# Gated linear attention and a hard-swish feed-forward on one core: output stores moved to the sync queue, and another order of all steps

## The chip, the cores and the metric

The kernel runs on one core of a Trainium2 chip. The metric is the device time in microseconds, as the median of several runs. The program is built on the host in one pass: a Python function issues instructions to five engines, and each engine executes its own instructions strictly in the order in which they were issued. The engines are TensorE (matrix products, called PE in the profile; its weight loads are PEld), VectorE (DVE), ScalarE (ACT), GpSimd (POOL) and SyncE (SP, which does nothing here but start transfers). They meet only through semaphores.

## The reference

Two blocks follow each other. The first is a recurrent attention with a decay for each channel; the second is a feed-forward block with a hard-swish gate. Inputs have 4 batches, 8 heads, 768 tokens and 48 channels a head; the second block sees 3072 tokens of 384 features, and has 2048 hidden features. The weights `w_in` and `w_out` arrive as float64.

```python
state = np.zeros((B, H, D, D))
for t in range(S):
    state = alpha[:, :, t, :, None] * state + np.einsum('bhd,bhe->bhde', k[:, :, t], v[:, :, t])
    y[:, :, t] = np.einsum('bhd,bhde->bhe', q[:, :, t], state)
x = y.transpose(0, 2, 1, 3).reshape(B * S, H * D)
h = x @ w_in
g = h * np.clip(h + 3.0, 0.0, 6.0) / 6.0
out = g @ w_out
```

## The kernel before, in words

**Tiling.** The 3072 tokens are cut into 24 chunks of 128 tokens (six a batch), and two chunks make a group of the feed-forward block (groups 0 to 11). In a chunk, the recurrence is written as matrix products: a running product of the decays (two scans on VectorE, steps `r` and `p`), scaled keys and queries (`k`, `q`), masked scores (`sc`, `m`), the product with the values (`yi`), the part that comes from the carried state (`yx`), and the update of that state (`u`, `sm`, `st`). Groups 0 and 1 (and group 0 in halves, by chunk) take the feed-forward block directly: `fa`, `fb` and `f` are the first product, `fr` and `fg` the gate, `b` the second product of group 0. From then on both products are done with fewer multiplications and more additions: `xc` and `y` form sums of inputs and weights, `M` are the twenty products of a group, `n` copies a product from PSUM, `o` sums them, `e` and `h` are the gate; `s` forms sums of gated values, `P` are the seven products of the second layer, `K` and `G` collect them, and `O` stores a quarter of the group's output.

**Weights.** [...] each weight is decoded from its two 32-bit words. The weights come in 16 slices (0 to 7 are `w_in`, 8 to 15 are `w_out`). Step `w.i` (function `load_weight`, line 172) loads slice i: four transfers for a slice of `w_in`, one for a slice of `w_out`. For slices 0 to 4, two of the four transfers are started from ScalarE's queue and two from SyncE's; all others are started from SyncE:

```python
queue = nc.scalar if i < 5 and p > 1 else nc.sync      # line 183
```

Decoding has four or five steps: `d1.i` (line 207) and `d2.i` (line 217) on ScalarE, `dx.i` (line 212) on ScalarE for slices 0, 1, 2 and 4 only, `d3.i` on VectorE (lines 224 to 231), and `d4.i` on GpSimd (line 238), after which the slice may be used. A slice i of `w_in` is what `fa.i`, `fb.i`, `f.0.i` and `f.1.i` multiply with. Raw words of slices 0, 1 and 2 have buffers of their own, which later slices use again; slices 3 and 4 lie in space that group 1's gated values take later.

**Loads and stores.** `la`, `lk`, `lq` and `lv` load decays, keys, queries and values of a chunk from SyncE's queue: one or two transfers for chunks 0 to 5, four (or eight for the values from chunk 8 on) later. `kw` and `kr` write keys to memory and read them back in another layout, also from SyncE. The results are stored by `so` (line 620, chunks 0 and 1) and `O` (line 817, groups 1 to 11: 44 stores), both from ScalarE's queue. A result lies in one of four small buffers (`oh`), which the next user may write when the store has landed.

**Order.** The order is written out by hand as one long string of 1665 words (from line 842). A word is a step with its chunk or group and its buffer: `d2.1` is `magnitude(1)`, `f.0.3.2` is the first product of group 0 with slice 3 into PSUM bank 2. The words are executed one by one, so the order of the words of one engine is the order of its instructions. Words of different engines beside each other say nothing about time; only the order on each engine and the semaphores do. `z.m.n` are n products of the identity that nobody uses, which keep TensorE busy while it has nothing else to do.

Of the kernel before, what the change touches and what calls it, by code (L numbers as in the profile page):

```python
# [8 lines left out]
FP = mybir.dt.float32  # L9
# [8 lines left out]
def kernel(  # L18
# [32 lines left out]
    nc = tc.nc  # L51
    B, H, S, D = q.shape
    NTOK, DM = out.shape
    C = 128
# [6 lines left out]
    G = 2  # L61
# [23 lines left out]
    v0 = consts.tile([C, H, 64], FP, tag="vfirst")  # L85
# [42 lines left out]
    st, sm = [], []  # L128
# [490 lines left out]
    def store(c):  # L619
        nc.scalar.dma_start(out=out[c * C : (c + 1) * C, :], in_=os_t.pop(c))  # L620
# [193 lines left out]
    def store2(g, i):  # L814
        row, col = PLACES[i]
        j = G * g + row
        nc.scalar.dma_start(out=out[j * C : (j + 1) * C, col * HD : (col + 1) * HD],
                            in_=oh_t.pop((g, i)))
# [17 lines left out]
    def run(words):  # L836
        for word in words.split():
            name, *at = word.split(".")
            steps[name](*(int(x) for x in at))

    with tc.manual_schedule():
        run("""la.0 z.3.5 lv.0.0 lk.1 lq.0 ta.0.0 lv.1.1 z.0.3 ca.0 r.0 lk.0 tk.1.1 la.1 p.0 tq.0.2
               z.0.8 la.2 q.0 lq.1 tk.0.3 z.0.2 k.0 lv.3.2 ta.1.0 sc.0.2.3 ca.1 la.3 r.1 ta.2.0 w.1
               z.0.3 ca.2 m.0 kb.0.0 z.0.2 ck.0 r.2 tq.1.2 yi.0.3 p.1 z.0.3 lq.2 cy.0 k.1 u.0.0 q.1
               lk.2 ta.3.3 sm.0 sc.1.1.2 ca.3 lk.3 p.2 d1.1 kb.1.0 w.0 m.1 st.1 d2.1 tq.2.3 dx.1
               z.0.1 q.2 yi.1.1 d3.1 tk.2.2 ck.1 yx.1 r.3 u.1.3 lq.3 cy.1 k.2 d4.1 tk.3.0 lv.2.0
               sm.1 sc.2.1.2 k.3 w.3 st.2 fa.1.0 d2.0 m.2 d1.0 kb.2.3 d3.0 fb.1 dx.0 p.3 tq.3.0 w.4
               z.1.2 ck.2 d4.0 q.3 fr.0.1.0 u.2.1 sc.3.2.3 fg.0.1 sm.2 fa.0.1 m.3 st.3 d2.3 d1.3
               kb.3.0 w.5 d3.3 fb.0 ck.3 u.3.1 fr.0.0.1 yi.3.2 d4.3 sm.3 d1.4 fg.0.0 yi.2.3 d2.4 w.2
               dx.4 yx.3 d3.4 yx.2 f.0.3.2 cy.3 d4.4 cy.2 d1.5 la.5 d2.5 f.1.3.3 fr.0.3.0 lq.5 d3.5  # L850
               la.4 d1.2 f.1.4.0 fg.0.3 lv.4.1 d4.5 d2.2 dx.2 w.6 d3.2 tq.5.0 fr.1.3.1 ta.4.1 d4.2
               fr.1.4.0 ta.5.2 fg.1.3 fa.4.1 ca.4 fg.1.4 ca.5 r.4 w.7 fa.2.2 r.5 f.0.5.3 p.4 d2.6
               d1.6 st.4 lq.4 fb.2 fr.0.5.1 d3.6 w.8 f.1.5.0 fr.0.2.0 d1.7 fg.0.5 d4.6 fg.0.2 d2.7
               tq.4.3 fr.1.5.1 f.1.0.3 d3.7 w.9 q.4 d4.7 f.1.6.2 fr.1.0.0 fg.1.5 d2.8 fg.1.0 p.5
               d1.8 w.10 f.1.7.0 d3.8 fr.1.6.1 d2.9 q.5 f.0.7.3 d4.8 d1.9 lk.4 fg.1.6 fr.1.7.0 d3.9
               w.11 f.0.6.2 fr.0.7.1 d2.10 fg.1.7 d4.9 d1.10 fg.0.7 tk.4.1 fr.0.6.0 d3.10 f.1.2.0
               w.12 k.4 d4.10 fb.4 fg.0.6 d2.11 fr.1.2.1 d3.11 sc.4.2.3 w.13 d1.11 fr.0.4.0 f.1.1.3
               fg.0.4 d4.11 m.4 d2.12 d1.12 kb.4.0 lk.5 d3.12 b.1.0.2 fr.1.1.0 ck.4 w.14 fg.1.1
               d4.12 d2.13 fg.1.2 b.0.0.1 d1.13 d3.13 w.15 u.4.1 tk.5.2 d4.13 sm.4 b.1.1 k.5 d2.14
               st.5 d1.14 d3.14 lq.6 sc.5.3.0 yi.4.1 m.5 lq.7 d4.14 b.1.2 d2.15 d1.15 d3.15 la.6  # L860
               yx.4 b.0.1 tq.6 d4.15 lv.5.2 y.6 la.7 b.1.3 y.5 y.1 y.7 lk.7 y.2 y.11 yi.5.2 bo.1 x.0
               so.1 b.0.2 lv.7.0 y.4 y.13 ca.6 yx.5 y.0 b.0.3 cy.5 r.6 la.8 bo.0 cy.4 x.1 y.3 lv.8.1
               P.1.0.3 s.1.0.0 s.1.1.1 P.1.3.0 xc.2.1 x.2 K.1.0 s.1.2.3 xc.2.3 tk.7 s.1.3.2 P.1.2
               K.1.1 y.10 y.8 P.1.1.2 y.9 y.16 xc.2.4 s.1.4 P.1.4 x.3 K.1.2 y.15 s.1.5 xc.2.5 P.1.5
               G.1.1.0 P.1.6 G.1.3.1 y.17 y.19 G.1.0.2 y.18 y.12 y.20 M.2.0.1 tq.7 G.1.2.3 M.2.15.2
               M.2.16 lv.6.2 n.2.0.8 xc.2.6 y.21 y.23 M.2.1 xc.2.0 lk.6 lq.8 tk.6 xc.2.7 M.2.7.0 k.6
               xc.2.8 ca.7 xc.2.9 xc.2.2 r.7 vh.8 n.2.1.9 M.2.2 O.1.2 n.2.7.10 o.2.4.0 p.6 ca.8 lq.9
               la.10 la.9 lk.8 lk.9 xc.2.10 kb.6.0 M.2.8 O.1.1 n.2.2.11 M.2.3 M.2.4 n.2.4.12 o.2.0.0
               k.7 y.14 q.6 e.2.0.0 h.2.0 M.2.18.3 M.2.17 M.2.5 n.2.5.13 ck.6 M.2.9 o.2.1.0 e.2.1.1
               kb.7.3 sc.6.2.1 M.2.10 ck.7 u.6.0 u.7.3 n.2.10.14 M.2.11 n.2.11.15 p.7 m.6 q.7  # L870
               sc.7.1.2 M.2.12 n.2.18.12 M.2.19 y.22 M.2.6.1 h.2.1 n.2.12.11 M.2.13 sm.6 r.8 y.24
# [140 lines left out]
```

## Time and profile before

| what | value |
|---|---|
| median of 3 runs (lowest to highest) | 555.63 us (554.13 to 557.94) |
| span of the profiled run | 554.3 us |
| instructions | 14864 |
| DVE busy | 474.6 us (86%) |
| ACT busy | 205.0 us (37%) |
| transfers | 52.82 MB, 95 GB/s in the mean |

An engine's row gives the time in which it executed something, its share of the span, and the number of its instructions. TensorE's row counts the `z` products too. The mean hides the stages: memory traffic is near 200 GB/s in the first 95 us, where the weights come in, and near 100 GB/s later; VectorE is above 90% from 110 to 350 us.

### The profile page before, as it was taken

The page shows a single profiled execution, that of the slowest core. Times are in us where ns is not written, and L with a number is a line of the kernel's source. Part 1 is how long each engine was busy: PE and PEld are TensorE (multiplying, and loading weights), DVE is VectorE, ACT ScalarE, POOL GpSimd, SP SyncE. Part 2 cuts the span into 40 slices and gives each one's busy share as a digit, 9 for nine tenths or more (in the row PEclk, how much of TensorE's full clock was granted, in tenths as well). Part 3 has the DMA queues.
Part 4 walks back from the last instruction along what each step waited for, and adds up shares of the span by engine and source line. Part 5 has one row for each costly group of instructions (what it writes and reads, how often), then busy time and mean ns, then how long its engine had stood idle before and what let it go on. Part 6 is the DMA issues. An engine that isn't in the chain of part 4 may idle for free.

```text
span 554.3 us, 14864 instructions
## 1 busy us (share of the span) xinstructions
PE 539.9 (97%) x6222; PEld 512.7 (93%) x6222; DVE 474.6 (86%) x822; ACT 205.0 (37%) x358; POOL 56.1 (10%) x76
## 2 busy tenths in 40 slices
PE   8989999999999999999999999999999999999997
PEld 8789886699999899899999999999899899999997
DVE  6978997999999999899999998897899678756381
ACT  2487672104342332252251343333324333233230
POOL 3334346000100000000100000000100100000000
PEclk9999999999999999999999999999999999999999
DMA  8998678232303355343444434053234310000001
GB/s 176 200 200 172 197 240 211 57 73 67 81 0 80 96 127 136 97 119 94 99 117 109 101 84 110 26 136 99 62 86 116 88 33 8 8 31 2 10 19 44
DMA packets 98515, 52.82 MB, mean 95 GB/s; under 512 B 51472, under 2 KB 91664, under 8 KB 98448
## 3 DMA queue, kind: packets, MB, share of 16 engines
q1 hardware_dynamic: 90704, 45.18, 34.5%
q10 hardware_dynamic: 7744, 6.69, 4.1%
q8 instruction: 49, 0.80, 0.6%
q14 instruction: 18, 0.15, 0.1%
HBM read 43.71 MB, written 8.13 MB: 94 GB/s over the span
## 4 chain that ended last, share of the span: by engine, by line
PE 84%; DVE 6%; DMA 5%; issue 2%; ACT 1%; SPq 1%; ACTq 0%; POOL 0%; DVEq 0%; POOLq 0%
PE m_ps L796 32%; PE m_ps L693 29%; PE m_ps L571 6%; PE m_ps L609 4%; PE t_ps L549 2%; DMA v<-in_v_dram 2%; DMA out_dram<-oh 2%; PE m_ps L582 1%; PE t_ps L383 1%; DVE g_sb L630 1%; PE t_ps L408 1%; PE t_ps L529 1%; PE t_ps L314 1%; PE t_ps L533 1%; PE m_ps L625 1%
## 5 line engine op out<-in xcount | busy, mean ns | idle before, releaser
L796 PE MATMUL m_ps<-w,g_sb 128*128 128x192 f32 x704 | 121.5, 326 | 0.0
L796 PEld LDWEIGHTS m_ps<-w,g_sb 128*128 128x128 f32 x704 | 113.8, 190 | 0.4
L699 ACT COPY g_sb<-m_ps 128x512 f32<-128x512 f32 x110 | 63.9, 584 | 130.5 <-PE m_ps L693 108.6
L796 PE MATMUL m_ps<-rings,g_sb 128*128 128x192 f32 x528 | 91.4, 326 | 0.0
L693 PE MATMUL m_ps<-xc,w 128*128 128x128 f32 x640 | 83.7, 278 | 2.0 <-DVE oh L812 1.2
L796 PEld LDWEIGHTS m_ps<-rings,g_sb 128*128 128x128 f32 x528 | 85.3, 190 | 0.2
L587 ACT ACTIVATE r<-g_sb,half 128x512 f32<-128x512 f32 x80 | 56.7, 722 | 73.2 <-DVE g_sb L634 41.9
L693 PEld LDWEIGHTS m_ps<-xc,w 128*128 128x128 f32 x640 | 78.0, 192 | 4.3 <-DVE oh L812 1.4
L591 DVE SCALAR_TENSOR_TENSOR g_sb<-r,g_sb 128x512 f32<-128x512 f32 x80 | 53.7, 681 | 5.5 <-ACT r L587 4.4
L471 POOL TENSOR_TENSOR t<-t,R 128x384 f32<-128x384 f32 x20 | 21.8, 1088 | 360.4 <-DVE t L509 153.7
L693 PE MATMUL m_ps<-xT,raw 128*128 128x128 f32 x400 | 51.6, 276 | 0.7 <-DVE g_sb L632 0.7
L693 PEld LDWEIGHTS m_ps<-xT,raw 128*128 128x128 f32 x400 | 48.3, 192 | 1.4 <-DVE g_sb L632 1.0
L740 DVE TENSOR_TENSOR g_sb<-g_sb 128x512 f32<-128x512 f32 (+1 forms) x55 | 42.7, 802 | 2.5 <-PE m_ps L796 2.3
L693 PE MATMUL m_ps<-xT,w 128*128 128x128 f32 x320 | 42.3, 276 | 0.0
L693 PEld LDWEIGHTS m_ps<-xT,w 128*128 128x128 f32 x320 | 39.5, 192 | 0.2
L630 DVE TENSOR_TENSOR g_sb<-g_sb 128x512 f32<-128x512 f32 x40 | 27.8, 700 | 7.4 <-ACT g_sb L699 7.4
L341 DVE TENSOR_TENSOR_SCAN R<-t,ones 128x516 f32<-128x516 f32 x24 | 30.0, 1249 | 3.4 <-ACT t L332 2.0
L571 PE MATMUL m_ps<-xT,w 128*128 128x256 f32 x144 | 32.3, 381 | 0.0
L693 PE MATMUL m_ps<-xc,raw 128*128 128x128 f32 x240 | 32.1, 277 | 0.0
L352 DVE TENSOR_TENSOR_SCAN P<-t 128x516 f32<-128x516 f32 x24 | 30.3, 1262 | 0.1
L571 PEld LDWEIGHTS m_ps<-xT,w 128*128 128x128 f32 x144 | 26.9, 190 | 3.7 <-issue 0.2
L693 PEld LDWEIGHTS m_ps<-xc,raw 128*128 128x128 f32 x240 | 29.6, 192 | 0.5 <-issue 0.2
(121 smaller groups left out, 740.3 us busy)
## 6 DMA issues: line engine op xcount, KB each, us to landing
raw<-in_moe_w_out_dram SPq DMA_DIRECT2D x8, 768.0 KB, 4.4
out_dram<-oh ACTq DMA_DIRECT2D x44, 96.0 KB, 2.1
raw<-in_moe_w_in_dram SPq DMA_DIRECT2D x18, 192.0 KB, 4.2
qq<-in_q_dram SPq DMA_DIRECT2D x36, 96.0 KB, 2.6
aq<-in_alpha_dram SPq DMA_DIRECT2D x36, 96.0 KB, 2.6
kq<-in_k_dram SPq DMA_DIRECT2D x36, 96.0 KB, 2.5
far<-kq SPq DMA_DIRECT2D x13, 256.0 KB, 2.1
kb<-far SPq DMA_DIRECT2D x52, 64.0 KB, 2.2
```

The source lines that it names most:

```text
L341: nc.vector.tensor_tensor_scan(out=reverse(R, n - 1, n), data0=reverse(ax, n, n), data1=reverse(ones, n, n), initial=0.0, op0=ALU.mult, op ...
L352: nc.vector.tensor_tensor_scan(out=P_t[j], data0=aX[j % 2][:, 0:n], data1=ini[j % 2], initial=0.0, op0=ALU.mult, op1=ALU.add)
L471: nc.gpsimd.tensor_tensor(out=st[j % 2], in0=sm[j % 2], in1=R_t[j][:, :, 0:1].to_broadcast([C, NP, 2 * D]), op=ALU.mult)
L571: nc.tensor.matmul(h[:, f], w1[:, kk, o : o + C], xT_t[g][:, kk], start=(kk == 0), stop=(kk == KT - 1))
L587: nc.scalar.activation(out=to, in_=h, func=AF.Relu, bias=half, scale=1.0 / 6.0)
L591: nc.vector.scalar_tensor_tensor(out=to, in0=r, scalar=1.0, in1=h, op0=ALU.min, op1=ALU.mult)
L609: nc.tensor.matmul(o_t[c], gs[0][:, f, c * C : (c + 1) * C], w2[:, f], start=(f == 0), stop=(f == NF - 1))
L630: eng.tensor_tensor(out=out, in0=in0, in1=in1, op=ALU.add if s1 > 0 else ALU.subtract)
L693: nc.tensor.matmul(acc[g][i][:, f * C : (f + 1) * C], spots[w][:, f * C : (f + 1) * C], x_of(g, x), start=(first and f == 0), stop=last, s ...
L699: nc.scalar.copy(out=slots[z], in_=acc[g][i])
L740: nc.vector.tensor_tensor(out=out, in0=in0, in1=in1, op=ALU.subtract)
L796: nc.tensor.matmul(to[g], a, rhs[:, f], start=(first and f == 0), stop=(last and f == HF - 1), skip_group_check=True)
```

## The change

Two things are changed, and a name is given to one tile.

1. The output stores `so` and `O` are started from SyncE's queue in place of ScalarE's. They were the only transfers besides the halves of weight slices 0 to 4 that ScalarE started. The aim is that ScalarE no longer stands behind a result that another engine has yet to write.
2. All 1665 words stand in another order. It is the same set of steps, with some PSUM banks and buffers given out differently, and with the same 29 idle products, most of which now stand before the second transposition of keys. In the opening, chunks 0 to 3 are taken one after the other with the decoding of a weight slice between them; slice 0 comes first, and slice 4 only after slice 9.

```diff
@@ stores @@
-        nc.scalar.dma_start(out=out[c * C : (c + 1) * C, :], in_=os_t.pop(c))
+        nc.sync.dma_start(out=out[c * C : (c + 1) * C, :], in_=os_t.pop(c))
...
-        nc.scalar.dma_start(out=out[j * C : (j + 1) * C, col * HD : (col + 1) * HD],
+        nc.sync.dma_start(out=out[j * C : (j + 1) * C, col * HD : (col + 1) * HD],
                             in_=oh_t.pop((g, i)))
@@ the opening @@
-        run("""la.0 z.3.5 lv.0.0 lk.1 lq.0 ta.0.0 lv.1.1 z.0.3 ca.0 r.0 lk.0 tk.1.1 la.1 p.0 tq.0.2
-               z.0.8 la.2 q.0 lq.1 tk.0.3 z.0.2 k.0 lv.3.2 ta.1.0 sc.0.2.3 ca.1 la.3 r.1 ta.2.0 w.1
-               z.0.3 ca.2 m.0 kb.0.0 z.0.2 ck.0 r.2 tq.1.2 yi.0.3 p.1 z.0.3 lq.2 cy.0 k.1 u.0.0 q.1
-               lk.2 ta.3.3 sm.0 sc.1.1.2 ca.3 lk.3 p.2 d1.1 kb.1.0 w.0 m.1 st.1 d2.1 tq.2.3 dx.1
-               z.0.1 q.2 yi.1.1 d3.1 tk.2.2 ck.1 yx.1 r.3 u.1.3 lq.3 cy.1 k.2 d4.1 tk.3.0 lv.2.0
-               sm.1 sc.2.1.2 k.3 w.3 st.2 fa.1.0 d2.0 m.2 d1.0 kb.2.3 d3.0 fb.1 dx.0 p.3 tq.3.0 w.4
-               z.1.2 ck.2 d4.0 q.3 fr.0.1.0 u.2.1 sc.3.2.3 fg.0.1 sm.2 fa.0.1 m.3 st.3 d2.3 d1.3
-               kb.3.0 w.5 d3.3 fb.0 ck.3 u.3.1 fr.0.0.1 yi.3.2 d4.3 sm.3 d1.4 fg.0.0 yi.2.3 d2.4 w.2
-               dx.4 yx.3 d3.4 yx.2 f.0.3.2 cy.3 d4.4 cy.2 d1.5 la.5 d2.5 f.1.3.3 fr.0.3.0 lq.5 d3.5
...
+        run("""la.0 z.3.5 lv.0.0 lk.1 lq.0 ta.0.0 lv.1.1 z.0.3 ca.0 r.0 lk.0 tk.1.1 z.0.2 z.0.2
+               z.0.1 z.0.8 tk.0.2 p.0 k.0 tq.0.3 q.0 la.1 ta.1.0 ca.1 r.1 k.1 sc.0.2.3 m.0 p.1
+               kb.0.0 ck.0 u.0.1 sm.0 yi.0.0 lq.1 la.2 ta.2.2 tq.1.3 q.1 z.0.2 kb.1.1 w.0 ca.2 r.2
+               cy.0 ck.1 d2.0 d1.0 dx.0 lk.2 tk.2.2 k.2 sc.1.0.3 m.1 z.0.3 w.1 d2.1 st.1 kb.2.1
+               yi.1.2 u.1.0 yx.1 z.0.3 d3.0 d4.0 sm.1 d3.1 lq.2 lv.2.2 tq.2.3 fa.0.0 cy.1 ck.2 d1.1
+               u.2.0 la.3 ta.3.2 p.2 q.2 sc.2.1.3 m.2 st.2 dx.1 d4.1 ca.3 r.3 p.3 fb.0 fa.1.1 fb.1
+               w.2 d2.2 d1.2 dx.2 fr.0.0.0 d3.2 d4.2 lk.3 lq.3 tk.3.2 k.3 tq.3.1 q.3 yi.2.3 yx.2
+               sm.2 st.3 sc.3.2.1 m.3 w.3 la.5 fr.0.1.1 d2.3 d3.3 fg.0.1 d1.3 d4.3 kb.3.0 fa.2.2
+               lv.3.0 yi.3.1 yx.3 cy.3 fb.2 ck.3 u.3.2 sm.3 la.4 fr.0.2.1 cy.2 ta.4.1 ca.4 fg.0.2
+               r.4 fg.0.0 w.5 d1.5 d2.5 d3.5 d4.5 w.6 d2.6 d3.6 ta.5.0 f.0.3.3 f.1.0.1 fr.1.0.1
...
+               f.1.6.2 fr.1.6.0 d1.8 ca.5 r.5 f.1.3.1 f.0.6.0 fr.0.3.1 d4.8 w.9 d2.9 fg.1.6 k.4
+               fg.0.3 p.5 d1.9 d3.9 d4.9 fr.0.6.0 w.4 d2.4 d3.4 d1.4 dx.4 d4.4 fg.0.6 f.1.5.2
+               sc.4.1.2 m.4 f.0.7.3 kb.4.0 f.1.7.0 w.10 d2.10 d3.10 fr.0.7.1 fg.0.7 d1.10 d4.10 ck.4
+               fr.1.7.0 lv.4.1 u.4.3 sm.4 st.5 fg.1.7 fr.1.5.1 fg.1.5 w.11 d2.11 fr.1.3.0 d3.11
...
@@ one place in the middle @@
+               xc.6.7 m.14 h.5.2 xc.6.6 e.5.3.0 P.4.6 G.4.3.1 M.5.19 o.5.5.0 h.5.3 M.5.17 M.6.0.3
+               P.5.1.0 ca.16 sm.13 st.14 n.6.0.13 M.6.1 n.6.1.12 P.5.0.1 e.5.4.1 M.6.2 vh.14 yi.14.2
+               u.14.1 yx.14 kt.15 tq.15 p.15 h.5.4 r.16 e.5.6.0 h.5.6 o.5.7.1 la.18 lq.17 xc.6.8
+               s.5.0.8 n.6.2.11 e.5.5.1 M.6.7.2 e.5.7.0 K.5.0 h.5.7 M.6.3 M.6.4 h.5.5 s.5.1.15
+               s.5.2.9 G.5.0.2 tk.16 k.16 n.6.7.10 M.6.8 P.5.3.0 n.6.4.14 o.6.0.0 M.6.9 M.6.5 q.15
+               s.5.3.8 s.5.4 O.4.1 lv.15.1 kw.15 lq.16 kr.15 P.5.2 o.6.1.0 e.6.1.0 n.6.5.15 cy.14
+               e.6.0.1 xc.6.9 p.16 kt.16 sm.14 tq.16 s.5.5 q.16 h.6.0 ca.18 st.15 M.6.18.3 M.6.10
...
@@ the end @@
-               s.11.5 G.11.0.1 K.11.1 O.10.0 P.11.4 K.11.2 G.11.1.0 P.11.5 G.11.2.2 O.11.2 G.10.3.3
-               O.11.0 O.10.3 O.11.1 P.11.6 G.11.3.3 O.11.3""")
+               G.10.3.0 s.11.4 P.11.4 G.11.0.2 O.11.0 s.11.5 K.11.2 P.11.5 G.11.1.1 O.11.1 P.11.6
+               G.11.3.2 O.10.3 O.11.3 O.9.0 G.11.2.1 O.11.2""")
```

## The prediction

> **What bounds the kernel now.** I read the page first, then TensorE's waits, then the stretches, then the opening in order of time. The page says whose work fills the span:
>
> ```profile
> PE 539.9 (97%) x6222; PEld 512.7 (93%) x6222; DVE 474.6 (86%) x822; ACT 205.0 (37%) x358; POOL 56.1 (10%) x76
> PE   8989999999999999999999999999999999999997
> ```
>
> TensorE is the bound: 14.4 us of 554.3 are not filled. The step multiset is unchanged, so its work is too, and a new order can only change the gaps and what stands in place of the idle products `z`. The waits for the whole span show who ends TensorE's gaps; each is small:
>
> ```profile
> PE t_ps L549 <- issue: 2.5, 2, 1.3
> PE t_ps L494 <- ACT kb L437: 1.8, 2, 1.4
> PE m_ps L693 <- DVE oh L812: 1.2, 1, 1.2
> PE t_ps L529 <- ACT v L399: 1.0, 1, 1.0
> PE m_ps L693 <- ACT g_sb L699: 0.8, 1, 0.8
> ```
>
> The stretches (columns: length, then busy us of PE, PEld, DVE, ACT, POOL, clock, transfers) tell where:
>
> ```profile
> 10.00:20.00 10.00, 9.85 (x130) 8.46 (x128) 9.04 (x14) 3.65 (x6) 1.42 (x1) 1.00 0.94 201
> 20.00:30.00 10.00, 9.03 (x134) 7.60 (x133) 8.80 (x16) 5.93 (x7) 3.73 (x3) 1.00 1.10 205
> 30.00:40.00 10.00, 8.58 (x184) 8.04 (x186) 8.80 (x15) 7.83 (x10) 4.14 (x3) 1.00 0.85 187
> 40.00:50.00 10.00, 10.00 (x69) 8.82 (x61) 7.08 (x10) 9.30 (x13) 4.54 (x3) 1.00 0.97 192
> 300.00:350.00 50.00, 50.00 (x582) 49.13 (x584) 46.62 (x82) 17.83 (x35) 1.68 (x2) 1.00 0.40 97
> ```
>
> From 40 us on TensorE is full but for 6.8 us between 160 and 450 and the end. In the first 40 us it is idle for 4.0 and does about 8 us of `z` (29 products; 16 records, eight products, took 1.95), so some 12 us are lost there, while transfers run at 200 GB/s. VectorE at 93% in the last row has little to give. The full stretch begins with the first whole `f`:
>
> ```profile
> 40.37 8.04 PE L571 MATMUL m_ps<-xT,w 128*128 128x256 f32 x36
> ```
>
> What holds the opening is the weights' way through ScalarE (ACTq is a transfer started from ScalarE's queue):
>
> ```profile
> 18.01 0.32 ACTq L184 DMA_DIRECT2D raw<-in_moe_w_in_dram  x1
> 18.30 0.93 ACT L207 ACTIVATE raw<-raw 128x768 int32<-128x768 uint32 x1
> 19.76 0.40 ACTq L184 DMA_DIRECT2D raw<-in_moe_w_in_dram  x1
> ...
> 27.62 0.90 ACT L217 ACTIVATE w<-raw 128x768 f32<-128x768 f32 x1 [3.84 <-DMA g_sb<-in_moe_w_in_dram]
> 28.42 0.92 ACT L207 ACTIVATE raw<-raw 128x768 int32<-128x768 uint32 x1
> 29.37 1.93 ACT L212 ACTIVATE raw<-raw 128x768 f16<-128x768 int32 x1
> 29.38 0.88 ACTq L184 DMA_DIRECT2D g_sb<-in_moe_w_in_dram  x2
> ```
>
> Slice 0's halves leave at 18.01 and 19.76, and ScalarE stands for 3.84 until `d2.0` can start at 27.62. The last two lines also show that a transfer is started when the instruction before it begins, not when it ends.
>
> **What the Trainium skill says.** "DMA: Bandwidth & Descriptors", section on issuing engines: transfers from the scalar and sync queues run on the same 16 engines and interleave, so another queue saves only issue time. The trace agrees: transfers fill 0.94 to 1.10 of the engines in the rows above, whichever queue starts them. The same page, anatomy of one DMA: a wait for a semaphore is done by the sequencer that issues, ahead of dispatch; so a store that waits holds the loads behind it on SyncE. Before, ScalarE did this waiting (it stood 3.7 us for `oh` at L812 once between 160 and 460). Its rules for authors: start early, wait late; the 3.84 above is that rule broken once. "TensorE: Matmul & The Clock Gate", Part 1: after an idle window of about 3.4 us the clock falls to half. Here the longest gap in TensorE's row is 1.5 and the clock is 1.00, so no run shows it yet.
>
> **The change, part by part.**
>
> *The opening.* Up to its first whole `f` (`f.0.3`), the new order places all that the old one does ahead of its own (`f.0.3` too, at 40.4), and further `fa.2`, `fb.2` (1.34 each, spacing of L582), `ta.4`, `ta.5` (0.45 each): 3.6 us. It breaks even if `f.0.3` starts at 44.0. It needs slice 3. The halves of slices 0 to 4 from ScalarE's queue now stand directly ahead of their own decoding: `dx.0, w.1, d2.1` and `dx.1, ca.3, w.2, d2.2`; in the old order four ScalarE instructions stood between the start of slice 1 and its first decoding step, and four again for slice 0. Each landing is thus shown in full, in series with ScalarE. Landings of these halves took 3.1 to 7.4 us, median 5.5 from ScalarE's queue in the windows at 10 and 18 us, 5.0 at 26.
>
> - `k.0` ends at 10.7 as before, `q.0` at 11.3, `sc.0` (1.1) and `kb.0` (0.45) at 12.9; `ck.0` starts at 13.0 and `w.0` leaves at 13.1; landed 18.7.
> - `d2.0`, `d1.0` (0.92 each) to 20.6; `dx.0` starts and `w.1` leaves, landed 26.6 (two issues 0.5, landing 5.5).
> - `d2.1`, `cy.1`, `ck.2` (0.92, 0.46, 0.67), `d1.1` (0.92) to 29.6; `dx.1` starts and `w.2` leaves; landed (5.0) 34.8.
> - `d2.2`, `d1.2` to 36.7; `dx.2` starts, `w.3` leaves, landed 41.7.
> - `d2.3` (0.92), `d3.3` on VectorE (0.69, 0.69, 0.96) and `d4.3` on GpSimd (1.84): 46.9.
>
> So `f.0.3` starts near 47, 3.0 later than break-even. Behind the waiting `d2.1` stand `ck.2` (for `u.2`) on ScalarE, and behind `d3.1` the scan `p.2` on VectorE. With landings of 3.1 from `w.1` on it is 41, but then VectorE and TensorE set it, near 44: 0; with 7.4 it is +9. I take +3.0.
>
> *Slice 4* is loaded late, again with `d2.4` next. `fg.0.6` on VectorE stands behind `d3.4`, `ck.4` behind all of slice 4 and slice 10. From the end of `f.0.6`: landing 4 to 5, `d2.4`, `dx.4`, two `d2`/`d1`, `fr.0.7` come to some 11 us until `ck.4`; TensorE has `f.1.5`, `sc.4`, `f.0.7`, `kb.4`, `f.1.7` (3 x 2.59 + 1.1 + 0.45 = 9.3) ahead of `u.4`. +1.2 (0 to 2.6).
>
> *Stores on SyncE.* 44 issues of 0.34 leave ScalarE, which is 37% busy; what they can give is TensorE's waits for ScalarE after 160, 1.0 + 0.8: I take -1.0. They come to SyncE, whose four-part load takes 2.0 and eight-part load of values 5.3 to 8.0. Between `tq.15` and `tq.16` the new order has six `M` (0.89) and two `P` (2.60) on TensorE, 10.6 us; SyncE has `lq.17`, `O.4.1`, `lv.15`, `kw.15`, `lq.16` (2.0 + 0.4 + 5.6 + 0.4 + 2.0) and 2.6 to landing, 13.0. Late by 2.4, and about 1 more at `lv.8` by the same reckoning. VectorE waits, and in its wake TensorE: +2.0 (0 to 5).
>
> *The end.* The old last copy waited 0.5 (551.33 against 550.79) for a store; the new one takes a free buffer, but two stores follow the third last on the queue (0.4 each): +0.3. The tile's name costs nothing, it is in no instruction. Moving the `z` products costs nothing either: they fill the wait for `lk.0`.
>
> Sum: 3.0 + 1.2 - 1.0 + 2.0 + 0.3 = +5.5, hence 561.1.
>
> **The rivals.**
>
> *Faster (0.12).* ScalarE and the new order close the gaps from 160 to 450 (6.8), and the opening breaks even: 555.6 - 6.8 + 0.3 = 549. For it: each gap is small and ended by an engine the change relieves or reorders. Against: only 1.8 of it waits for ScalarE, and VectorE is as full as before.
>
> *Hidden (0.25).* Landings are short because SyncE has run out of other loads, slice 4 is covered, loads are in time: +0.3 to +2, about 556.5. For it: in the old trace transfers fall to a third of the engines near 33 us. Against: the 3.84.
>
> *A cold clock (0.11).* Between `fa.0` (about 25.8) and `u.2` (behind `ck.2`, 28.7) TensorE has 3 us with nothing; if this passes the skill's window, small products run at half speed for another such window, and with landings of 7.4: 555.6 + 9 + 2 + 3 = 569 at the outside.
>
> **How the numbers follow.** The main case has 0.52 and spreads over 556 to 567 about 561.1. 1% is 5.6 us, so 550.1 and 561.2 part the classes. The unknown costs of the main case reach further up (+9, +2.6, +5) than down, so I put 0.6 of it (0.31) above 561.2; with the cold clock that is 0.42 for slower. Same gets the rest of it and the hidden case, 0.46, and faster 0.12. The range of 552 to 569 leaves out most of the fast rival and what lies beyond the cold one.
>
> **What would show it.** In the changed profile: ScalarE's L217 waiting for a transfer of `raw` two to three times for 3 us or more in the first 45 us; the first L571 near 47; a gap at L494 near 28; small gaps near 80; VectorE's L318 waiting for `qq` near 300; ACT without waits for L812. The prediction is wrong if L571 starts before 44, or if TensorE's gaps after 160 sum to less than 4.

## The result, and the profile after

The changed kernel takes 563.4 us in the median of four runs (562.3 to 564.2), against 555.9 us (554.1 to 557.9) for the kernel before on the same chip: a ratio of 1.0132, 95% interval 1.0091 to 1.0174, so slower by about 1.3%. The profiled run has a span of 560.9 us, 6.6 more than before. Three views say where the 6.6 us went. First the page: the engines' row for TensorE, and the granted clock in 40 slices of 14 us.

```profile
PE 543.6 (97%) x6222; PEld 515.8 (92%) x6222; DVE 473.7 (84%) x822; ACT 203.8 (36%) x358; POOL 53.2 (9%) x76
PEclk9979999899999999999999999999999999999999
```

TensorE has the same 6222 products but is busy for 3.7 us more than before: the clock row has a 7 and an 8, slices in which the same work took longer. The stretches (from and to, length, then busy us of PE, PEld, DVE, ACT, POOL, clock, share and rate of the transfers) put the first of them into the opening:

```profile
10.00:20.00 10.00, 8.82 (x123) 7.55 (x122) 9.28 (x15) 2.73 (x5) 0.84 (x1) 1.00 1.17 218
20.00:30.00 10.00, 6.19 (x116) 5.02 (x113) 4.13 (x8) 5.90 (x7) 2.62 (x2) 1.00 1.11 219
30.00:40.00 10.00, 8.63 (x67) 8.11 (x62) 7.11 (x10) 5.69 (x6) 1.83 (x1) 0.66 0.89 198
40.00:50.00 10.00, 10.00 (x188) 9.02 (x187) 6.53 (x12) 5.49 (x10) 4.16 (x3) 1.00 0.71 156
```

Between 20 and 30 us TensorE is busy for only 6.2 us of 10 and VectorE for 4.1, where before they were at 9.0 and 8.8. So it is neither of them that sets the pace there. The two engines' own instructions say what they wait for: the timeline of ScalarE (its transfers are ACTq, the bracket is the idle time ahead and its releaser), then one line of VectorE's and TensorE's gaps with the first `f`:

```profile
13.54 0.86 ACTq L184 DMA_DIRECT2D raw<-in_moe_w_in_dram  x2
20.12 0.93 ACT L217 ACTIVATE w<-raw 128x768 f32<-128x768 f32 x1 [1.78 <-DMA raw<-in_moe_w_in_dram]
21.95 0.80 ACTq L184 DMA_DIRECT2D raw<-in_moe_w_in_dram  x2
27.83 0.89 ACT L217 ACTIVATE w<-raw 128x768 f32<-128x768 f32 x1 [3.94 <-DMA rings<-in_alpha_dram]
30.83 0.81 ACTq L184 DMA_DIRECT2D raw<-in_moe_w_in_dram  x2
37.03 0.91 ACT L217 ACTIVATE w<-raw 128x768 f32<-128x768 f32 x1 [4.25 <-DMA raw<-in_moe_w_in_dram]
38.80 0.92 ACTq L184 DMA_DIRECT2D g_sb<-in_moe_w_in_dram  x2
43.48 0.92 ACT L217 ACTIVATE w<-g_sb 128x768 f32<-128x768 f32 x1 [1.75 <-DMA g_sb<-in_moe_w_in_dram]
```

```profile
28.75 0.69 DVE L224 TENSOR_SCALAR w<-w 128x768 f32<-128x768 f32 x1 [5.63 <-ACT w L217]
```

```profile
25.85 1.60 PE L582 MATMUL m_ps<-xT,w 128*128 128x128 f32 x12 [1.63 <-POOL w L238]
29.63 0.56 PE L494 MATMUL t_ps<-v,kb 128*48 128x48 f32 x16 [2.18 <-ACT kb L437]
32.16 2.08 PE L408 MATMUL t_ps<-q,k 48*128 48x128 f32 x16 [1.37 <-DVE q L364]
...
50.21 13.12 PE L571 MATMUL m_ps<-xT,w 128*128 128x256 f32 x60
...
80.41 2.86 PE L571 MATMUL m_ps<-xT,w 128*128 128x256 f32 x12 [1.40 <-DVE g_sb L591]
83.69 0.56 PE L494 MATMUL t_ps<-v,kb 128*48 128x48 f32 x16 [0.42 <-ACT kb L437]
...
109.28 1.93 PE L539 MATMUL t_ps<-A,v 128*32 128x128 f32 x32 [2.81 <-DVE A L416]
```

Four pairs of ACTq and L217: half of a slice is started, and 4.7 to 6.6 us later its first decoding step begins. ScalarE has three short copies to do behind the first start, nothing behind the second and one or two instructions behind the others; for the rest it stands idle, 1.78, 3.94, 4.25 and 1.75 us. The releaser of 27.83 names another load; it is inferred, and what `d2.1` reads is slice 1. Behind this `d2.1` stand VectorE (5.63 us, for what `d2.1` writes) and then TensorE at 29.63 and 32.16; its gap ahead of 25.85 belongs to slice 0, whose last step `d4.0` was over only then (23.97 + 1.82). The first `f` comes at 50.21; at 44.0 the opening would have broken even.

The third view is TensorE's row of waits over the whole span (sum, times, longest):

```profile
PE t_ps L494 <- ACT kb L437: 3.3, 3, 2.2
PE t_ps L539 <- DVE A L416: 2.8, 1, 2.8
PE t_ps L408 <- DVE q L364: 1.9, 2, 1.4
```

The three longest rows are all made ahead of 110 us. Of the waits that stood at L693 and L529 before, none is left: behind 160 us the gaps sum to 0.7 us (0.23 and 0.48), where they were 6.8. So the new order loses in the first 136 us and wins in the rest:

| part | after against before, us |
|---|---|
| opening: first `f` at 50.21, even at 44.0 | +6.2 |
| gaps at 80 and 84 us (before: none) | +1.8 |
| gaps at 109 and 136 us (2.81, 0.17; before: none) | +3.0 |
| low clock from 110 to 114 us (2.0 at 0.50, 2.0 at 0.81) | +1.4 |
| gaps behind 160 us, 0.7 for 6.8 | -6.1 |
| from the last product's end to the end, 3.9 for 3.5 | +0.4 |
| sum (the spans differ by 6.6) | +6.7 |

The opening's share is that of one pair of profiles. Two other runs below have the same opening in the same order, with the first `f` at 50.71 and 51.85, so it is good to a microsecond or two.

### The profile page after: what moved, and what is told of

It is laid out like the page before. It is cut to its first block, busy times and chain, and to the rows that moved or that the text cites. A ratio compares the mean times of both kernels' runs of the same rounds, so it can differ in the third digit from the quotient of the medians.

```text
span 560.9 us, 14905 instructions
## 1 busy us (share of the span) xinstructions
PE 543.6 (97%) x6222; PEld 515.8 (92%) x6222; DVE 473.7 (84%) x822; ACT 203.8 (36%) x358; POOL 53.2 (9%) x76
## 4 chain that ended last, share of the span: by engine, by line
PE 75%; DVE 4%; DMA 2%; issue 1%; POOL 1%; ACT 1%; POOLq 0%; DVEq 0%; ACTq 0%
PE m_ps L796 33%; PE m_ps L693 33%; DMA raw<-in_moe_w_out_dram 2%; PE t_ps L549 2%; PE t_ps L383 2%; PE t_ps L529 2%; PE t_ps L533 1%; PE t_ps L488 1%; DVE rings L740 1%; POOL w L238 1%; PE t_ps L385 1%; DVE raw L630 1%; PE t_ps L539 0%; DVE raw L634 0%; ACT w L217 0%
## 5 line engine op out<-in xcount | busy, mean ns | idle before, releaser
L699 ACT COPY g_sb<-m_ps 128x512 f32<-128x512 f32 x110 | 63.6, 586 | 139.0 <-PE m_ps L693 120.0
L693 PE MATMUL m_ps<-xc,w 128*128 128x128 f32 x640 | 83.1, 277 | 0.0
L693 PEld LDWEIGHTS m_ps<-xc,w 128*128 128x128 f32 x640 | 78.1, 192 | 0.9 <-issue 0.2
L693 PE MATMUL m_ps<-xT,raw 128*128 128x128 f32 x400 | 52.1, 277 | 0.0
L471 POOL TENSOR_TENSOR t<-t,R 128x384 f32<-128x384 f32 x20 | 20.2, 1008 | 330.0 <-DVE t L509 192.1
L693 PEld LDWEIGHTS m_ps<-xT,raw 128*128 128x128 f32 x400 | 48.4, 192 | 0.8 <-issue 0.2
L693 PE MATMUL m_ps<-xT,w 128*128 128x128 f32 x320 | 42.5, 277 | 0.0
L693 PEld LDWEIGHTS m_ps<-xT,w 128*128 128x128 f32 x320 | 39.4, 192 | 0.7 <-issue 0.2
L693 PE MATMUL m_ps<-xc,raw 128*128 128x128 f32 x240 | 32.0, 276 | 0.0
L693 PEld LDWEIGHTS m_ps<-xc,raw 128*128 128x128 f32 x240 | 29.5, 192 | 0.6 <-issue 0.6
L630 DVE TENSOR_TENSOR g_sb<-m_ps,g_sb 128x512 f32<-128x512 f32 x30 | 20.6, 685 | 10.7 <-PE m_ps L693 6.3
```

What stands on the lines that cost most here:

```text
L471: nc.gpsimd.tensor_tensor(out=st[j % 2], in0=sm[j % 2], in1=R_t[j][:, :, 0:1].to_broadcast([C, NP, 2 * D]), op=ALU.mult)
L630: eng.tensor_tensor(out=out, in0=in0, in1=in1, op=ALU.add if s1 > 0 else ALU.subtract)
L693: nc.tensor.matmul(acc[g][i][:, f * C : (f + 1) * C], spots[w][:, f * C : (f + 1) * C], x_of(g, x), start=(first and f == 0), stop=last, s ...
L699: nc.scalar.copy(out=slots[z], in_=acc[g][i])
```

## The experiments

Ratios are against the kernel before, in runs on the same chip as each experiment.

### The stores' queue in the new order

```diff
-        nc.sync.dma_start(out=out[...
+        nc.scalar.dma_start(out=out[...
```

> The changed kernel with the output stores back on ScalarE's queue, order kept. Theory (the new order closed TensorE's gaps after 160 us, 6.8 to 0.7): gaps stay under 2, time 562 to 565. Rival (the queue of the stores closed them): gaps of 4 us or more come back, time 567 to 570.

575.0 us, ratio 1.0342 (1.0306 to 1.0377), 11.6 more than the changed kernel and more than either theory gave. Behind 160 us TensorE's gaps sum to 8.1 us in place of 0.7, so the order alone had not closed them. TensorE's waits have a new first row, and ScalarE's timeline shows one of its causes:

```profile
PE m_ps L693 <- ACT g_sb L699: 7.0, 4, 4.3
```

```profile
455.95 0.34 ACTq L817 DMA_DIRECT2D out_dram<-oh  x1
456.34 0.72 ACT L587 ACTIVATE r<-g_sb,half 128x512 f32<-128x512 f32 x1 [5.93 <-DVE oh L812]
456.96 0.57 ACT L699 COPY g_sb<-m_ps 128x512 f32<-128x512 f32 x1
```

The store that leaves at 455.95 had stood in ScalarE's row for the `oh` that VectorE had yet to write (5.93 us of idle time); behind it stands the copy at L699, which empties the bank that TensorE needs. The new order puts stores well ahead of their data; where SyncE does this waiting, as in the changed kernel, TensorE's 0.7 us of gaps show no cost.

### The stores' queue in the old order

```diff
-        nc.scalar.dma_start(out=out[...
+        nc.sync.dma_start(out=out[...
```

> The kernel before with the output stores on SyncE's queue alone, order kept. Theory (the queue matters little by itself): 554.5 to 558, gaps after 160 us of 5 to 8. Rival (the queue closes the gaps): 549 to 551. The prediction's fear (stores hold loads back on SyncE): 558 or more.

567.4 us, ratio 1.0208 (1.0165 to 1.0251): the time of the prediction's fear (558 or more), though it is a store that waits behind loads and not a load behind stores. One gap of 8.0 us that ends at 244 us and the clock after it (0.50 from 244 to 248 us) make most of the loss. ScalarE's line and SyncE's queue:

```profile
243.98 0.32 ACT L809 COPY oh<-m_ps 128x192 f32<-128x192 f32 x1 [10.50 <-DMA out_dram<-oh]
```

```profile
235.88 5.32 SPq L299 DMA_DIRECT2D v<-in_v_dram  x8
...
241.88 1.92 SPq L817 DMA_DIRECT2D out_dram<-oh  x4
```

The store stands behind the eight parts of a value load, the copy at L809 waits for its buffer, and L693 for the copy. Of the loss 3.1 us lies in the opening, where nothing was changed (first `f` at 43.48 against 40.37): openings of one order differ by so much between runs. So neither half of the change stands alone: moving the stores costs 12 us in the old order, the new order costs 12 us more without it. Neither queue is better by itself; the order has to be laid out for the queue that the stores are on.

### Late halves in the old order

The halves from ScalarE's queue were made a step of their own, `wa.i`, and put right ahead of the decoding of their slice in the old order: `wa.1` ahead of `d1.1`, `wa.0` of `d2.0`, `wa.3` of `d2.3`, `wa.4` of `d1.4`, `wa.2` of `d1.2`.

```diff
-            for p in range(NP):
-                queue = nc.scalar if i < 5 and p > 1 else nc.sync
+            for p in (range(2, NP) if second else range(2 if i < 5 else NP)):
+                queue = nc.scalar if second else nc.sync
```

> The kernel before, with the ScalarE-started halves of slices 0 to 4 each started right ahead of its own first decoding step on ScalarE, as the changed kernel has them; nothing else moves. Theory (late starts cost the opening): the first L571 at 44 to 48 us in place of 40.4, time 559 to 563. Rival: under 557, since transfers fill the memory engines anyway.

567.8 us, ratio 1.0214 (1.0168 to 1.0260): 12.6 us for five starts moved back, more than the theory gave. The first `f` comes at 45.75, 5.4 us later, as the theory said. ScalarE stands 5.58 and 5.86 us for the first steps of two slices, and TensorE behind it:

```profile
27.38 0.88 PE L494 MATMUL t_ps<-v,kb 128*48 128x48 f32 x16 [4.83 <-ACT kb L437]
...
52.64 7.69 PE L571 MATMUL m_ps<-xT,w 128*128 128x256 f32 x23 [4.03 <-ACT xT L557]
```

The late start alone is enough, in the old order, to lose what the change lost and more.

### Early halves in the new order, from ScalarE

The same split in the changed kernel, with `wa.0 wa.1` behind `w.0`, `wa.2 wa.3` behind `dx.0` and `wa.4` behind `ca.4`.

> The changed kernel, with the ScalarE-started halves of slices 1, 2, 3 and 4 started earlier on ScalarE (1 right behind 0, 2 and 3 behind dx.0, 4 behind ca.4); nothing else moves. Theory (the late starts make the opening's loss): the first L571 at 44 to 46 us in place of 50.2, no stretch at half clock near 33 us, the gap at 80 us gone, time 556 to 559. Rival (the chunk-by-chunk order, VectorE or memory traffic sets the opening, and the waits for landings only show it): L571 stays at 49 or later, time 562 or more.

559.9 us, ratio 1.0082 (1.0043 to 1.0121). The gaps at 80 us are gone, but the first `f` comes at 51.02, no earlier than in the changed kernel. That looks like a verdict against the late starts; the timeline of ScalarE shows that it isn't one:

```profile
12.87 5.68 ACTq L184 DMA_DIRECT2D raw<-in_moe_w_in_dram  x4
```

```profile
24.73 3.62 ACTq L184 DMA_DIRECT2D g_sb<-in_moe_w_in_dram  x2
28.45 0.89 ACT L217 ACTIVATE w<-raw 128x768 f32<-128x768 f32 x1 [4.32 <-DMA g_sb<-in_moe_w_in_dram]
```

In the changed kernel two such starts took 0.80 to 0.92 us; here it was 5.68 us from the first of four to the end of the last, and 3.62 us for two. ScalarE stood at the issue, and `d2.1` began 0.10 us after the issue was over. The wait for a landing had only been exchanged for a wait at the issue, at the same place. Slices 2 and 3 did come in time (`d2.2` starts at 33.33 without a wait), and TensorE has no gap from 32.77 us on; but its clock is 0.50 from 32 to 38 us, as in the changed kernel from 32 to 36, and `f` comes no earlier. How much of that is the stand ahead of `d2.1`, and how much the clock behind it, this run doesn't part. It mixed several things and left the question open; the next one is cleaner.

### All parts from SyncE's queue

```diff
-                queue = nc.scalar if i < 5 and p > 1 else nc.sync
+                queue = nc.sync
```

> The changed kernel with one line different: all four parts of slices 0 to 4 are started from SyncE's queue, at the places where SyncE's own two parts stand (8.7, 10.4, 16.1 and 20.3 us in the changed kernel's trace), so that ScalarE starts nothing and can't stand at an issue[...]. The same bytes move. Theory A (the late start of ScalarE's halves is what makes the opening long; starting them early from ScalarE had only put the issue's standing in place of the wait for the landing): the waits of 3.9 and 4.3 us ahead of d2.1 and d2.2 fall below 1.5, VectorE no longer stands 5.6 us ahead of d3.1, TensorE's gaps between 25 and 33 us (5.2) shrink to under 2.5 and with them the stretch at half clock; the first L571 comes at 44 to 47 us instead of 50.2, and the time is 557 to 561. Theory B (the opening is bound by the bytes of all loads, whichever is started first): the loads of chunks 2 and 3 come later by what the halves come earlier, new waits for k, q or v of chunk 2 take their place, the first L571 stays at 49 to 52, and the time is 562 to 565.

552.7 us, ratio 0.9958 (0.9941 to 0.9975), where the changed kernel had 1.0132: 1.7% less, or about 10 us (the two medians, from two chips, differ by 10.7), from one line that moves no byte less. SyncE's queue (slices 1 and 3), then ScalarE's L217 for slices 1, 2 and 3, then TensorE's first `f`:

```profile
11.04 2.12 SPq L184 DMA_DIRECT2D raw<-in_moe_w_in_dram  x4
...
24.05 4.78 SPq L184 DMA_DIRECT2D g_sb<-in_moe_w_in_dram  x4
```

```profile
21.10 0.94 ACT L217 ACTIVATE w<-raw 128x768 f32<-128x768 f32 x1
...
28.14 0.91 ACT L217 ACTIVATE w<-raw 128x768 f32<-128x768 f32 x1 [0.96 <-DMA raw<-in_moe_w_in_dram]
...
33.50 0.98 ACT L217 ACTIVATE w<-g_sb 128x768 f32<-128x768 f32 x1 [0.24 <-DMA g_sb<-in_moe_w_in_dram]
```

```profile
42.64 13.12 PE L571 MATMUL m_ps<-xT,w 128*128 128x256 f32 x60
```

Issues take as long here (2.12 and 4.78 us for four), but an engine stands at them that computes nothing. The waits of 3.94, 4.25 and 1.75 are down to none, 0.96 and 0.24; the clock is 1.00 throughout; the first `f` is 7.6 us earlier. The spread is small too: 552.0 to 553.9 in 20 runs, where the kernel before had 553.1 to 559.0 in 23. Theory A holds in the waits that it named, also against the reading of the run before it; the first `f` and the time came out better than it gave (44 to 47, 557 to 561). The two profiled spans differ by 9.4 us: the opening gives 7.6, the gaps at 80 us 1.8 and the clock at 110 us 1.4, and the gaps near 109 us take 0.6 back. Those stay in another form, 3.6 us between 99 and 126 us for 3.0, so they belong to the order and not to the halves.

### One slice at a time

```diff
-                queue = nc.scalar if i < 5 and p > 1 else nc.sync
+                queue = nc.scalar if i in (0, 2, 3, 4) and p > 1 else nc.sync
```

> The changed kernel with the parts of slice 1 alone all on SyncE; slices 0, 2, 3 and 4 keep their halves on ScalarE. It tells how the late starts add up. Theory A (each late landing costs by itself: slice 1's holds ScalarE's kb, VectorE's decoding and by the gaps the clock, 5 to 6 us; slices 2 and 3 some 2 more): the wait ahead of d2.1 and the half clock go, the waits ahead of d2.2 and d2.3 stay at 2 to 5 us, the first L571 comes at 45 to 47, the time is 557 to 560. Theory B (the latest of them alone sets the end, slice 3's landing): the opening hardly moves, the first L571 at 49 to 50.5, 562 to 564.

561.9 us, ratio 1.0104 (1.0045 to 1.0163), with runs from 559.2 to 563.3; the profile is of the lowest. In it `d2.1` has no wait, the opening keeps its clock, `d2.2` and `d2.3` still wait 4.60 and 3.21 us, and the first `f` comes at 46.33. So the opening behaved as theory A says, and the time of the median does not: 1.5 us of about 10. How much slice 1 is worth alone is not settled beyond "a part, and not all".

```diff
-                queue = nc.scalar if i < 5 and p > 1 else nc.sync
+                queue = nc.scalar if i == 4 and p > 1 else nc.sync
```

> The changed kernel with the parts of slices 0 to 3 on SyncE, and slice 4's half on ScalarE as in the changed kernel, started right ahead of its own decoding. Against the run with all five on SyncE (552.7) it gives the price of slice 4 alone. Theory A (my step for slice 4: 1.2, 0 to 2.6; the changed kernel's trace had gaps of 1.40 and 0.42 at 80 us behind a wait of 4.6): ScalarE waits 4 us or more for it near 70 us, TensorE's gaps of 1.4 to 2 us stand there again, and the time is 554 to 555. Theory B (those gaps were VectorE's, or the opening's delay carried on): no gap, 552 to 553.3.

555.8 us, ratio 1.0008 (0.9987 to 1.0029), against 0.9958 with slice 4 on SyncE too: 0.5%, or 2.8 us, for slice 4. ScalarE's lines and TensorE's:

```profile
65.32 0.87 ACTq L184 DMA_DIRECT2D g_sb<-in_moe_w_in_dram  x2
70.83 0.91 ACT L217 ACTIVATE w<-g_sb 128x768 f32<-128x768 f32 x1 [4.84 <-DMA g_sb<-in_moe_w_in_dram]
```

```profile
73.83 2.86 PE L571 MATMUL m_ps<-xT,w 128*128 128x256 f32 x12 [1.61 <-DVE g_sb L591]
77.09 0.56 PE L494 MATMUL t_ps<-v,kb 128*48 128x48 f32 x16 [0.40 <-ACT kb L437]
```

The two gaps, 2.0 us, are slice 4's. Theory A's wait and gaps are there, at a somewhat higher price than it gave; the two intervals leave that price open by more than a microsecond.

### Is it an error of the new order?

The same line (all parts from SyncE's queue) in the old order, its stores left on ScalarE.

> The kernel before (old order, stores from ScalarE) with the same one line: all four parts of slices 0 to 4 from SyncE's queue. It tells whether the gain of 10.7 us that this line brought in the new order comes from an error of the new order or from something that both orders pay. Theory A (the new order's placing of the halves was the error; the old one had placed them ahead of need, and stood at an issue or a landing for 3.8 us once): the first L571 moves by under 1.5 us from 40.4, and the time is 554 to 557. Theory B (transfers started from ScalarE cost in any order, by standing at the issue): the first L571 comes 2 to 4 us earlier and the time is 551 to 553. Third, the old order's loads on SyncE are placed for two parts each, and with four the loads of k and v of chunks 2 and 3 come late: the first L571 at 42 to 45, 557 to 561.

553.4 us, ratio 0.9969 (0.9952 to 0.9986). The first `f` comes at 38.43, 1.9 us earlier, and the time falls by 1.3: between theories A and B. The old order paid a little for its starts from ScalarE, the new one about 10 us. With the halves on SyncE the two orders can't be told apart (0.9958 and 0.9969, intervals overlapping). Behind 160 us the new one has 1.0 us of gaps for 6.7, but between 99 and 126 us it has 3.6 us where the old one has none. So the verdict on the change is this: new order and moved stores together are worth nothing measurable once the halves are out of the way, and what they cost is the place of those starts.

### Was it the clock?

```diff
-  lq.2 lv.2.2 tq.2.3 fa.0.0 cy.1 ck.2 d1.1 u.2.0 la.3 ta.3.2 p.2 q.2 sc.2.1.3
+  lq.2 lv.2.2 tq.2.3 z.1.6 fa.0.0 z.1.9 cy.1 ck.2 d1.1 u.2.0 la.3 ta.3.2 p.2 q.2 z.1.5 sc.2.1.3
```

> The changed kernel with 20 more idle products on TensorE in the opening's three gaps: six ahead of fa.0, nine behind it, five ahead of sc.2 (0.24 us each: 1.5, 2.2 and 1.2 us, the sizes of the gaps). No landing changes; results are unchanged. Theory A (the stretch at clock 0.50 between 31 and 37 us is made by those gaps, and TensorE is the bound from 32 us on): the clock stays at 1.00, the first L571 comes 2 to 3 us earlier, at 47 to 48 us, and the time is 560 to 562. Theory B (the slow clock costs nothing, because slice 2's and slice 3's landings at 37.0 and 43.5 us set the opening): the clock stays at 1.00 but the first L571 stays at 49.5 to 50.5 with new gaps ahead of d2.2's and d2.3's users, and the time is 563 to 564.

562.3 us, ratio 1.0124 (1.0064 to 1.0183): not to be told from the changed kernel. The clock stayed at 1.00 up to 40 us, and the first `f` came at 51.80, later than either theory gave. ScalarE waits 5.39 us for slice 2 (38.77), a new gap stands on TensorE, and behind it the clock falls after all (0.50 from 44 to 46 us):

```profile
42.41 1.16 PE L408 MATMUL t_ps<-q,k 48*128 48x128 f32 x16 [1.75 <-DVE q L364]
...
51.80 13.12 PE L571 MATMUL m_ps<-xT,w 128*128 128x256 f32 x60
```

```profile
40.00:45.00 5.00, 3.25 (x48) 2.58 (x39) 4.22 (x8) 3.76 (x5) 2.41 (x2) 0.85 0.64 152
45.00:50.00 5.00, 5.00 (x78) 4.68 (x77) 2.94 (x4) 2.38 (x4) 1.70 (x2) 0.81 0.91 192
```

So the slow stretch was moved and not removed, and slice 2 could be decoded 1.7 us later than in the changed kernel. The run speaks for theory B, since TensorE, with its products twice as fast, only came sooner to the next wait; but it doesn't isolate the price of the clock. Two other figures bound it. In the changed kernel slice 3 landed at 43.48 us; with the durations of its decoding steps in that trace, and VectorE free at once, it would have been ready near 48.4 (an estimate; it was ready at 48.97). So a full clock could have brought the first `f` forward from 50.21 by 1.8 us at most. And in the two other runs with this opening the first `f` came at 51.85 with the clock at 0.50 from 28 to 30 and near 0.5 to 0.6 from 44 to 48 us (stores back on ScalarE), and at 50.71 with the clock at 0.50 from 26 to 38 us (`m.5` moved, below): it doesn't follow the length of the slow stretch. In the changed kernel TensorE is without a gap from 32 to 50 us and looks like the bound. A full row of an engine at half clock is no proof that it is.

### The gap at 109 us

`m.5` moved ahead, from behind `d4.14` to right behind `d3.13`.

```diff
-  d2.13 d3.13 s.1.3.2 w.14 d2.14 d3.14 d1.13 d4.13 d1.14 d4.14 m.5 lk.6
+  d2.13 d3.13 m.5 s.1.3.2 w.14 d2.14 d3.14 d1.13 d4.13 d1.14 d4.14 lk.6
```

> The changed kernel with one step at another place in the order: m.5 (the mask on the scores of chunk 5, VectorE's L416) stands right behind d3.13 and ahead of s.1.3 and the decoding of slice 14, where the changed kernel has it behind them. Theory A (TensorE's gap of 2.81 us at 109 us and the half clock behind it come from VectorE's order alone): the gap and the stretch at half clock go, nothing new takes their place, and the time is 559.5 to 561. Theory B (VectorE is full there, 9.8 of 10 us, and what is taken from m.5 is given to the next step that TensorE waits for): gaps of the same sum stand between 105 and 130 us behind another releaser, and the time is 562 to 564.

564.9 us, ratio 1.0181 (1.0130 to 1.0232). The gap is gone, and three others stand in its place, 4.4 us together:

```profile
110.45 5.40 PE L609 MATMUL m_ps<-w,g_sb 128*128 128x384 f32 x16 [1.57 <-DVE g_sb L591]
118.34 4.14 PE L609 MATMUL m_ps<-w,g_sb 128*128 128x384 f32 x12 [0.77 <-POOL w L238]
127.13 4.52 PE L796 MATMUL m_ps<-rings,g_sb 128*128 128x192 f32 x16 [2.05 <-DVE rings L740]
```

Theory B, at a time a little above its range: VectorE is full from 100 us on (9.83 of 10 in the changed kernel between 100 and 110), and with this step served first TensorE waits for others. One step was moved; that no other order of VectorE's steps would help is not shown.

### Two attempts at a faster kernel

With all parts on SyncE, the last eight idle products of the opening (1.95 us) were left out:

> The changed kernel with all parts of slices 0 to 4 on SyncE, and without the last eight idle products of the opening (two ahead of kb.1, three ahead of w.1, three ahead of d3.0: 1.95 us of TensorE's row). They fill waits or they delay. Theory A (with early landings TensorE is the bound from 17 us on): the first L571 comes 1 to 2 us earlier, near 41, and the time is 551 to 552. Theory B (they fill waits for k, q and the decoding, which end when they end): gaps stand in their place, the first L571 stays within 0.5 us of 42.6, and the time is 552 to 553.5. If the gaps add up to more than about 3 us in a row of 6, the clock may fall to half and the time is 554 to 556.

552.3 us, ratio 0.9953 (0.9935 to 0.9971); the first `f` at 42.82, not earlier than 42.64, and gaps of 0.69 and 0.54 us in their place. Theory B: they fill waits. The lowest time of the study, but not to be told from the run with them. The expectation's 3 us of gaps in 6 fit the changed kernel, where TensorE was busy for 2.6 us of the 6 from 26 to 32 us and the low clock followed. No run shows it to be a threshold: in the run with idle products the clock fell to 0.50 behind one gap of 1.75 us.

Last, the old order up to its 352nd step, and the steps that are left in the new order:

> Both orders in one: up to the 352nd step (near 150 us) the old order, from there the steps that are left in the new order, stores on SyncE as in the changed kernel, and all parts of slices 0 to 4 from SyncE's queue. Theory A (the new order's gain lies behind 160 us, where the old order with its SyncE halves still had 6.7 us of gaps and the new one 0.6; its loss lies ahead of 160 us, where the old order has none and the new one 3.7 beyond the opening; the two are separate): the first L571 at 38 to 39, under 1 us of gaps from 40 us to the last 30, and the time is 546 to 549. Theory B (the new order's full stretch behind 160 us rests on the waits that it had taken ahead of it, so that VectorE, which is 95% busy there, is now behind and the gaps come back): 2 to 5 us of gaps between 160 and 350 us, and the time is 550 to 553.

At the seam the two orders give out PSUM banks differently: `M.2.18` opens the bank in which `M.2.7` to `M.2.14` still sum, so group 2's first products are mixed there and this kernel's output is wrong. The instructions and their sizes are the same, so its time may be read as a sketch of such a kernel. 553.6 us, ratio 0.9938 (0.9914 to 0.9963). The first `f` is at 38.26, there is no gap from 40 to 130 us and none from 160 to 488; two gaps stand right behind the seam, which lies near 129 us, with a mean clock of 0.97 from 100 to 160 us:

```profile
131.05 1.28 PE L408 MATMUL t_ps<-q,k 48*128 48x128 f32 x16 [1.85 <-DVE q L364]
143.16 1.16 PE L693 MATMUL m_ps<-xT,w 128*128 128x128 f32 x8 [1.40 <-ACT g_sb L699]
```

Neither theory's time came true; the gaps are not where theory B put them, but most of the hoped-for gain was given back. A seam without the shared bank was not tried.

## Why the prediction was right, and where it was not

It gave 561.1 us in a range of 552 to 569; 563.4 came. What happened, slower by over 1%, had been given 0.42, a little less than no change. The time is right for a reason that is half right: against its terms the trace has +3.2 us in the opening, +0.6 at slice 4, +4.4 near 109 us and -7.1 for the stores and the gaps behind 160 us. That these misses cancel to +1.2 is luck.

- *The opening: right in mechanism, too small.* It said that the halves stand right ahead of their own decoding, so that each landing shows in series with ScalarE. The run with all parts on SyncE and the one with late halves in the old order show this to be the cause; the clock behind the gaps adds at most 1.8 us by the estimate above. The dates of the chain were close: `w.0` to `w.3` were to leave at 13.1, 20.6, 29.6 and 36.7 us and left at 13.54, 21.95, 30.83 and 38.80. (`w.2` stands behind `ca.3`, which needs `ta.3` from TensorE; it left 0.04 us behind the end of `ta.3` at 30.79, though `ca.3` itself began at 32.11 only.) The first `f` was put at 47 (+3.0) and came at 50.21 (+6.2). The lag at the last landing was 1.8 us (43.48 for 41.7); the other 1.5 came between that landing and `f` (6.7 us for 5.2). In that stretch `d3.3` waited 0.6 us for VectorE, and when slice 3 was ready at 48.97 TensorE still had 1.2 us of other products ahead of `f`: the sum of bare durations left both out. The Trainium skill's "DMA: Bandwidth & Descriptors", rules for kernel authors, says to issue a transfer early and to wait for it late; what the opposite costs here is the 10 us or so of the one-line run, slice 4 included.
- *The wait behind `d2.1`: right.* `ck.2` on ScalarE and the scan behind `d3.1` on VectorE stood as said: gaps of 2.18 us at L494 and 1.37 at L408, and VectorE idle for 5.63.
- *Slice 4: too small.* +1.2 (0 to 2.6) was said, though its own figures, 11 less 9.3, give 1.7; gaps of 1.8 us were in the trace, and the run that isolates it says about 2.8.
- *The gaps at 109 us and the low clock behind them: not seen, +4.4.* No step of the prediction looked at VectorE between 100 and 160 us; its 93% between 300 and 350 was all that was named. Moving one of VectorE's steps there did not help.
- *Stores on SyncE: wrong in sign.* -1.0 for ScalarE and +2.0 for late loads were said, +1.0 in all; the gaps behind 160 us went from 6.8 to 0.7. The term for ScalarE was read from the two waits that name it, as if the rest of the old waits would stay in a new order. The late loads did not show: VectorE has no wait for `qq` or `v` in the changed kernel. The estimate took each load's issue and landing in series, and it treated the queue and the order as two changes with a price each. The two runs that swap the queue of the stores show that they go together: in the old order stores on SyncE cost more than had been feared, in the new one they cost nothing that shows. This is where the prediction's own condition, gaps behind 160 us below 4, says that it was wrong.
- *The end: right.* +0.3 said, +0.4 found.
- *The rivals.* The faster case needed an even opening; its other half, the closing of the 6.8 us, came true. The hidden case falls with the waits of 3.94 and 4.25. The cold clock came in part: 0.50 from 32 to 36 us, worth at most 1.8 us by the same estimate. Its outside case sums to 569.6, not 569.
- *Two readings of the kernel before.* The rows that were read as transfers filling 0.94 to 1.10 of the engines have a 0.85 and a 0.40 among them. And the 3.84 us ahead of `d2.0` were taken for a landing; but the halves of slice 3 stand between in ScalarE's queue, and their start was over at 27.44, 0.18 us before `d2.0` began at 27.62. So ScalarE may have stood at an issue there already; which of the two it was isn't settled.

```profile
25.48 1.96 ACTq L184 DMA_DIRECT2D g_sb<-in_moe_w_in_dram  x2
```

## What to carry to other kernels

A transfer started from a computing engine's queue has two costs that a busy share doesn't show: started late, its landing stands in series with that engine, and started early, several together, the engine can stand at the issue (5.68 us for four here). Where another queue's engine computes nothing, as SyncE here, try starting the loads there before reordering a kernel: it is one line. And judge a new order stage by stage: here it won 6 us in the steady part and lost 12 up to 136 us, and most of the loss had a cheap cure.

## What was not expected of the hardware

- Issuing a transfer can hold an engine up for long. Two starts took 0.80 to 0.92 us on ScalarE in the changed kernel; in the early-halves run four took 5.68 us from first to last, and two 3.62. That it is the issue which holds the engine is in no trace line of its own: it shows as idle time of ScalarE that ends with the issue. What the issue itself waits for isn't shown.
- The clock falls after shorter gaps than the Trainium skill's "TensorE: Matmul & The Clock Gate", Part 1, leads one to expect (an idle window of about 3.4 us): it was 0.50 from 32 us after gaps of 1.63, 2.18 and 1.37 us, and at 110 us after a single one of 2.81, as these stretches of the changed kernel show, and in the run with idle products at 44 us after a single one of 1.75. A gap of 2.06 us at 99 us in the run with all parts on SyncE left it at 1.00. So it is not the length of one gap alone; what else decides isn't settled here.

```profile
32.00:34.00 2.00, 1.84 (x16) 1.78 (x16) 0.10 (x1) 0.78 (x2) 1.56 (x1) 0.50 1.09 216
...
110.00:112.00 2.00, 2.00 (x44) 1.93 (x40) 1.77 (x3) 0.00 (x0) 0.51 (x3) 0.50 0.14 39
```

- VectorE's L228 took 1.82 us once (at 105.21, beside GpSimd's L238 from 104.83 to 106.62), where its median is 0.62. The run with all parts on SyncE has the same pair (1.82 us at 95.05, beside L238 from 94.67 to 96.46). That one slows the other was not tested.
